# Whole plain groups beside the making of input sums, values x scores in alternating halves, and low parts of weights on VectorE

## The chip, the cores and the metric

One Trainium2 chip, one of its cores. The metric is the device time of the program in microseconds: 606.63 us in the median of three runs (605.3 to 607.45).

## What is computed

Three layers in a row, all in float32. First a decaying causal attention over 2 batches, 8 heads, 768 positions and 64 channels, in blocks of 64 positions:

```python
intra = einsum('bhic,bhjc->bhij', qb, kb) * Dmask          # Dmask = lam^(i-j), lower triangle
intra = einsum('bhij,bhjd->bhid', intra, vb)
inter = einsum('bhid,bhde->bhie', qb * lam_pow, kv_state)
out   = intra + inter
kv_state = lam_block * kv_state + einsum('bhsd,bhse->bhde', kb * rev_pow, vb)
```

Its output, as 1536 tokens of 512 features, goes through two layers of the same shape (512 to 2048 to 512):

```python
h = x @ w_in;  g = h * tanh(softplus(h));  x = g @ w_out      # first layer, mish
h = x @ w_in;  g = h * sigmoid(h);         out = g @ w_out    # second layer, silu
```

## The kernel before, in words

**Numbers in two parts.** TensorE multiplies float32 in a fast form that keeps the high bits of each operand. Every operand of the two layers is therefore held as a high part (a cast by ScalarE, L178, L402, L475) and a low part (the rest, a subtraction of the high part: L179 for weights, L403 for activations, L478 for x), and a product is three passes: high x high, low x high, high x low. The names end in h and l: `xh`/`xl` for the input tokens, `wh`/`wl` for weights, `th`/`tl` for differences of weights, `gh`/`gl` for activations, `sh`/`sl` for sums of inputs. Weights come as 64-bit numbers and are made into 32-bit ones by five VectorE instructions a tile (`split_op`, L122 to L138; in the second layer ScalarE does the first, L94).

**Tiles.** Tokens come in three tiles of 512 (t = 0, 1, 2), the 2048 hidden features of a layer in 16 slices of 128 (n), four slices to a group. There are eight groups, 0 to 7, four for each layer. A pair p is two slices, 2p and 2p + 1. `emit_h` (L418) makes the hidden values of one slice and one token tile in 12 matmuls into one PSUM bank, `activate` (L399 to L403) its activation with high and low part, `emit_o` (L441) multiplies it by the output weights in 12 matmuls into four banks that add up over a group, and `evac` (L457) adds the four banks to the output sums. Here an `emit_h` or an `emit_o` is called an item.

**Seven products instead of eight.** For token tiles 0 and 1 and a pair, the product of a 2 x 2 block matrix of x and a 2 x 2 block matrix of weights is made with seven block products instead of eight (class `Block`, L528 to L594, products by L549, six matmuls each). This needs four sums of the inputs (`sums`: made by `make_sums`, L508, for the first layer and at the end of `evac`, L487 to L502, for the second, in steps kept in the list `summing`), four differences of each pair's weights (`sum_pair`, L164), a copy of bank a to bank b by ScalarE (L568), a copy of the fifth product (L573), and two bank additions by VectorE (L557). Pairs in `plain` (L82) go without: their hidden values are made by `emit_h`, 4 items a pair. Before the change pairs 2 and 8 are plain: the first pair of group 1 and of group 4, while the sums of the layer are being made.

**Order.** The order of every engine's work is written out by hand; each engine runs its instructions in that order. The attention (12 chunks of 128 tokens; `emit_S` scores, `emit_state` state products, `emit_O` values x scores at L350 and state x queries at L344) runs first, its last eight chunks between the items of group 0 (loop at L635). Then, for each group from 1 to 7, the list `items` (L704 to L710) is gone through. After each item come, in this order: the weight parts that were pending when the item began (`run_parts`, L173: the cast by ScalarE, the low part), one low part of x (`run_rest`), one step of the sums (`run_sums`), k split instructions of the queue `todo` (`run_split`, k from L722 to L726), and weight loads into free slots (`pump`, on SP's queue). An activation's cast and low part come at the start of the next item (`run_later`).

Group 1 and group 4 (`first`, L699) begin with four `emit_h` of the plain pair, each followed by one of `fill`: an output item left over from the group before (group 1 has two of these and two idle places) with the split of an output weight queued behind it. Then follow the seven products of the second pair with output items between them. The other groups hold two pairs of seven products.

The lines that the change touches: `plain` L82; the low part of weights L179; the loops over halves and pairs in `emit_O` L348 to L352; the parts of x and the steps of the sums in `evac` L474 to L502 and in `make_sums` L520 to L526; the last attention step L643; the lists of the groups L684 to L724.

Of the kernel before, what the change touches and what calls it, by code (L numbers as in the profile page):

```python
# [7 lines left out]
F32 = mybir.dt.float32  # L8
# [9 lines left out]
def decay_attention_mish_silu_kernel(  # L18
# [60 lines left out]
    parts = []  # L79

    pre = []
    plain = (2, NF // 2)  # L82
    silu = []
    uses = {}

# [87 lines left out]
    def run_parts(k=None):  # L173
        for _ in range(len(parts) if k is None else min(k, len(parts))):
            hi, lo, f, key = parts.pop(0)
            ready.add(key)
            used(key)
            nc.scalar.copy(hi, f)  # L178
            nc.gpsimd.tensor_tensor(out=lo, in0=f, in1=hi.bitcast(F32), op=ALU.subtract)  # L179

    def run_split(k):
        for _ in range(min(k, len(todo))):
# [155 lines left out]
    def emit_O(n):  # L338
        c = n % CPS
        vn = nat.pop(n)[3]  # L340
        px = ps_a.tile([P, NP, C], F32, tag="a", name="px")
        if c > 0:
            for p in range(NP):
                nc.tensor.matmul(  # L344
                    px[:, p, :], lhsT=states[n % 2][:, p, :], rhs=qd[n][:, p, :],
                    start=(p == 0), stop=False, skip_group_check=True,
                )
        for hh in range(2):  # L348
            for p in range(NP):
                nc.tensor.matmul(  # L350
                    px[64 * hh : 64 * hh + 64, p, :], lhsT=vn[:, 2 * p + hh, :], rhs=sm[n][:, hh, p, :],
                    start=(c == 0 and p == 0), stop=(p == NP - 1), skip_group_check=True,  # L352
                )
        xslots.append(held.pop(("x", n)))
        xh, xl = x_tile(n // CPB)
        o = slice((n % CPB) * C, (n % CPB + 1) * C)
        xf = wk.tile([P, T], F32, tag="wa", name="xf").rearrange("p (a c) -> p a c", a=NP)
        nc.scalar.copy(xf, px)
        nc.scalar.copy(xh[:, :, o], xf)  # L359

        def finish():
            (nc.vector if n < PH else nc.gpsimd).tensor_tensor(out=xl[:, :, o], in0=xf, in1=xh[:, :, o].bitcast(F32), op=ALU.subtract)

        return finish
# [82 lines left out]
    def cast(i, f):  # L447
        return lambda: nc.scalar.copy(sums[i][0], f)
# [8 lines left out]
    def evac(mm, g, t):  # L457
        if g == 0:
            accs[mm, t] = (accp if t == 0 else late[1]).tile([P, 4, T], F32, tag="acc", name="acc")
        acc = accs[mm, t]  # L460
        for j in range(4):
            if g == 0:
                nc.scalar.copy(acc[:, j, :], po[t][j])
            else:
                nc.vector.tensor_tensor(out=acc[:, j, :], in0=po[t][j], in1=acc[:, j, :], op=ALU.add)  # L465
            if g == NG - 1 and mm == 1:
                r0 = t * T + j * P
                nc.sync.dma_start(out[r0 : r0 + P, :], acc[:, j, :])
        if g < NG - 1 or mm == 1:
            return  # L470

        xh, xl = x_tile(t)

        def part(j):  # L474
            nc.scalar.copy(xh[:, j, :], acc[:, j, :])  # L475
            rest.append((
                (t, j),
                lambda: nc.gpsimd.tensor_tensor(  # L478
                    out=xl[:, j, :], in0=acc[:, j, :], in1=xh[:, j, :].bitcast(F32), op=ALU.subtract
                ),  # L480
            ))

        if t != 1:
            for j in range(4):
                part(j)
            return
        a1, a2 = accs[0, 0], acc  # L487

        f1 = late[0].tile([P, 2, T], F32, tag="t4", name="s1", bufs=1)
        f3, f4 = a2[:, 0:2], a1[:, 2:4]  # L490
        add, sub = ALU.add, ALU.subtract
        drain = lambda: run_rest(len(rest))
        summing.extend([
            [tt(f1, a2[:, 0:2], a2[:, 2:4], add)],
            [cast(0, f1), lambda: part(0), lambda: part(1)],
            [low(0, f1), lambda: part(2), lambda: part(3), tt(f1, f1, a1[:, 0:2], sub)],
            [drain, cast(1, f1), tt(f4, f4, f1, sub)],
            [low(1, f1), tt(f3, a1[:, 0:2], f3, sub)],
            [cast(2, f3)],
            [low(2, f3)],  # L500
        ])
        last_sum.append([cast(3, f4), low(3, f4)])  # L502
# [5 lines left out]
    def make_sums():  # L508

        x0, x1 = x_tile(0), x_tile(1)  # L510
        sh, sl = [late[0].tile([P, 3, 2, T], F32R, tag=t, name=t, bufs=1) for t in ("sh", "sl")]
        sums.extend((sh[:, i], sl[:, i]) for i in range(3))
        sums.append((x1[0][:, 0:2], x1[1][:, 0:2]))
        q = lambda xt, k: [xt[i][:, 2 * k : 2 * k + 2].bitcast(F32) for i in (0, 1)]
        a11, a12, a21, a22 = q(x0, 0), q(x0, 1), q(x1, 0), q(x1, 1)
        tmp = late[1].tile([P, 4, T], F32, tag="acc", name="tmp")
        f1, f2 = tmp[:, 0:2], tmp[:, 2:4]
        f3 = late[0].tile([P, 2, T], F32, tag="t4", name="s3", bufs=1)
        add, sub = ALU.add, ALU.subtract
        summing.extend([  # L520
            [tt(f1, a21[0], a22[0], add), tt(f1, f1, a21[1], add), tt(f1, f1, a22[1], add), tt(f2, f1, a11[0], sub)],
            [cast(0, f1), tt(f2, f2, a11[1], sub), tt(f3, a11[0], a21[0], sub), tt(f3, f3, a11[1], add), low(0, f1)],
            [cast(1, f2), tt(f1, a12[0], f2, sub), tt(f1, f1, a12[1], add), tt(f3, f3, a21[1], sub), low(1, f2)],
            [cast(2, f3), low(2, f3)],
        ])
        last_sum.append([cast(3, f1), low(3, f1)])  # L526

    class Block:  # L528

# [105 lines left out]
    for i, (t, f) in enumerate(steps):  # L635
# [6 lines left out]
            make_sums()  # L642
        if i == len(steps) - 1:  # L643
            split_pair(3)
            sum_pair(3)
        for half in halves.get(i, ()):
            split_w(*half)
        if n < N:
# [29 lines left out]
    for g in range(1, 2 * NG):  # L678
        n0 = g * GF
        pa = n0 // 2  # L680
        A, B = Block(pa), Block(pa + 1)
        o = lambda t, f, a=False, b=False: lambda: emit_o(t, n0 + f, a, b)

        os = [(0, 0), (0, 1), (0, 2), (0, 3), (1, 1), (1, 0), (1, 3), (1, 2)]  # L684
        if g == 1:
            os = os[4:] + os[:4]
        os = [o(t, f, i % 4 == 0, i % 4 == 3) for i, (t, f) in enumerate(os)]
        hs = [lambda n=n0 + f: emit_h(2, n) for f in range(GF)]
        sp = lambda fn, *a: lambda: fn(*a)
        more = pa + 2 < NF  # L690
        nxt = [[lambda p=p: split_pair(p)] if p < NF else [] for p in (pa + 2, pa + 3)]
        if nxt[0]:
            nxt[0].append(lambda: sum_pair(pa + 2))
        fill = [[fn, sp(split_w, n0 + j, 1)] for j, fn in enumerate(fills + [idle] * (4 - len(fills)))]
        first = g in (1, NG)
        if g > 1:
            fill[0].append(lambda: sum_pair(pa + 1))
        fill[3] += nxt[0]
        if first:  # L699

            order = ((1, 1), (1, 0), (0, 0), (0, 1)) if g == 1 else ((0, 0), (0, 1), (1, 1), (1, 0))
            ha = [[lambda t=t, n=n0 + f: emit_h(t, n)] for t, f in order]
            ha[1 if g == 1 else 3].append(lambda: summing.append(last_sum.pop()))
            items = [it for i in range(4) for it in (ha[i], fill[i])]  # L704
        else:
            items = [[A.m1], [A.m5], fill[0], [A.m2], [A.m6], fill[1], [A.m7], [A.m3], fill[2], [A.m4], fill[3]]
        items += [
            [B.m1], [B.m5], [B.m2], [B.m6], [os[0]], [B.m7], [B.m3], [os[1]], [B.m4], [os[2]], [os[3]],
            [hs[0]], [os[4]], [hs[1], *nxt[1]], [os[5]], [hs[2]], [os[6]], [hs[3]], [os[7]],
        ]  # L710
        for at, item in enumerate(items):
            if g == NG and at == 7:
                silu.append(True)
            run_later()
            k = len(parts)
            for fn in item:
                fn()
            run_parts(k)
            run_rest(0 if g == NG and 7 <= at < 14 else 1)
            run_sums(1)  # L720
            small = isinstance(getattr(item[0], "__self__", None), Block)
            k = 1 if small else 0 if item[0] is idle else 3 if item[0] in hs or at < (18 if first else 11) else 2  # L722
            if g == NG and at < 8:
                k = (0, 1, 1, 1, 1, 3, 3, 3)[at]  # L724
            elif g == NG - 1 and at == len(items) - 1:
                k = 0  # L726
            run_split(k)
            pump()
        fills = [lambda n=n0 + f: emit_o(2, n, n % GF == 0, n % GF == GF - 1) for f in range(GF)]
# [49 lines left out]
```

## Time and profile before

| what | value |
|---|---|
| median of three runs | 606.63 us (605.3 to 607.45) |
| profiled execution, its own time | 607.67 us |
| its span, first to last instruction | 605.9 us |
| TensorE busy (matmul) | 575.0 us, 95% |
| VectorE busy | 418.2 us, 69% |
| ScalarE busy | 239.2 us, 39% |
| GpSimd busy | 325.5 us, 54% |
| mean granted TensorE clock | 0.979 |

The profile is one execution. PE is TensorE's matmuls, PEld its weight loads, DVE is VectorE, ACT ScalarE, POOL GpSimd, SP the engine that issues the loads. A group of instructions is named by line, engine, operation and tiles (out<-in). In brackets behind a row of a timeline stands how long the engine had been idle before it, and which instruction ended that. The duration of a matmul overlaps the next one's, so the pace of TensorE is read from starts, not from durations.

### The profile page before, as it was taken

To read this page: it belongs to the slowest core of one execution; us is meant where nothing else is said; L and a number is where in the kernel's file an instruction comes from. 1 tells how busy PE (TensorE), PEld (TensorE's weight loads), DVE (VectorE), ACT (ScalarE), POOL (GpSimd) and SP (SyncE) were. 2 spreads that over 40 slices of the span, in tenths; PEclk is the share of its full clock that TensorE was granted. 3 is DMA by queue.
4 is the path that set the end of the run, shared out by engine and by line. 5 is a ranking of instruction groups with operands and counts; after the bars stand their busy time and mean duration, and the time that the engine had idled before them with its cause. 6 is when DMAs were issued, how large, how long until landed. Compare 5 with 4: busy or idle time off the path is not lost. (4 is left out here: it accounts for less than half of the span.)

```text
span 605.9 us, 7515 instructions
## 1 busy us (share of the span) xinstructions
PE 575.0 (95%) x2870; PEld 469.3 (77%) x2870; DVE 418.2 (69%) x520; ACT 239.2 (39%) x439; POOL 325.5 (54%) x237
## 2 busy tenths in 40 slices
PE   7899999997899999999999859999999999999997
PEld 4777778886678888888887647788788878888886
DVE  3898963799858687768797779838834895567102
ACT  2435442436413334324426244446433542353220
POOL 1758783346446365646494548737554646445320
PEclk8999999999989999999999879999999999999999
DMA  7955720012322122312221112222402131200103
GB/s 253 421 179 165 288 70 1 1 35 70 104 67 73 36 69 76 98 36 70 70 70 36 35 35 70 69 70 70 133 6 70 46 102 62 70 1 1 70 0 138
DMA packets 14627, 50.55 MB, mean 83 GB/s; under 512 B 1528, under 2 KB 3072, under 8 KB 13312
## 3 DMA queue, kind: packets, MB, share of 16 engines
q1 hardware_dynamic: 14592, 50.08, 24.3%
q8 instruction: 22, 0.36, 0.2%
q14 instruction: 13, 0.11, 0.1%
HBM read 46.92 MB, written 3.15 MB: 83 GB/s over the span
## 5 line engine op out<-in xcount | busy, mean ns | idle before, releaser
L403 POOL TENSOR_TENSOR gl<-wa,gh 128x512 fp32r<-128x512 f32 x96 | 143.8, 1504 | 130.6 <-ACT gh L402 49.1
L179 POOL TENSOR_TENSOR wl<-dec,wh 128x512 fp32r<-128x512 f32 x64 | 88.4, 1381 | 84.9 <-ACT wh L178 84.8
L465 DVE TENSOR_TENSOR acc<-po,acc 128x512 f32<-128x512 f32 x72 | 46.4, 685 | 73.8 <-PE po L441 73.8
L399 ACT ACTIVATE wa<-ph 128x512 f32<-128x512 f32 x48 | 28.8, 599 | 154.2 <-PE ph L418 138.6
L441 PE MATMUL po<-gh,wh 128*128 128x512 f32 x192 | 76.8, 400 | 1.3 <-ACT wh L178 1.3
L418 PE MATMUL ph<-xl,wh 128*128 128x512 f32 x192 | 73.8, 392 | 4.0 <-POOL xl L478 4.0
L441 PE MATMUL po<-gh,wl 128*128 128x512 f32 x192 | 76.1, 396 | 0.9 <-POOL wl L179 0.9
L138 DVE SCALAR_TENSOR_TENSOR dec<-slot,dec 128x512 uint32<-128x512 uint32 x64 | 74.8, 1168 | 1.9
L418 PE MATMUL ph<-xh,wh 128*128 128x512 f32 x192 | 75.7, 394 | 0.2 <-ACT xh L359 0.2
L441 PE MATMUL po<-wl,gh 128*128 128x512 f32 x192 | 74.8, 390 | 0.9 <-POOL wl L179 0.9
L441 PE MATMUL po<-wh,gl 128*128 128x512 f32 x192 | 74.7, 389 | 0.0
L441 PE MATMUL po<-wh,gh 128*128 128x512 f32 x192 | 74.7, 389 | 0.0
L132 DVE TENSOR_SCALAR dec<-dec 128x512 f32<-128x512 f32 x64 | 47.4, 740 | 34.7 <-ACT dec L94 33.6
L136 DVE SCALAR_TENSOR_TENSOR dec<-slot,dec 128x512 uint32<-128x512 uint32 x64 | 60.6, 947 | 2.1
L402 ACT CAST gh<-wa 128x512 fp32r<-128x512 f32 x96 | 58.4, 623 | 1.1
L178 ACT CAST wh<-dec 128x512 fp32r<-128x512 f32 x64 | 39.6, 619 | 44.7 <-DVE dec L138 44.7
L418 PE MATMUL ph<-xh,wl 128*128 128x512 f32 x192 | 53.5, 393 | 0.0
L441 PE MATMUL po<-gl,wh 128*128 128x512 f32 x192 | 51.9, 392 | 0.0
L134 DVE TENSOR_SCALAR dec<-dec 128x512 uint32<-128x512 uint32 x64 | 49.7, 777 | 2.0
L179 POOL TENSOR_TENSOR tl<-t,th 128x512 fp32r<-128x512 f32 x24 | 33.6, 1408 | 24.6 <-ACT th L178 21.0
L418 PEld LDWEIGHTS ph<-xl,wh 128*128 128x128 f32 x192 | 36.0, 188 | 13.0 <-POOL xl L478 5.7
L441 PEld LDWEIGHTS po<-gh,wh 128*128 128x128 f32 x192 | 36.7, 191 | 10.3 <-ACT wh L178 1.7
(106 smaller groups left out, 962.2 us busy)
## 6 DMA issues: line engine op xcount, KB each, us to landing
slot<-w SPq DMA_DIRECT2D x64, 512.0 KB, 3.7
xslot<-x SPq DMA_DIRECT2D x10, 1024.0 KB, 9.0
out<-acc SPq DMA_DIRECT2D x12, 256.0 KB, 2.1
xslot<-x SPq DMA_DIRECT2D x4, 512.0 KB, 4.4
dmask<-scr SPq DMA_DIRECT2D x2, 256.0 KB, 4.5
lamrow<-scr SPq DMA_DIRECT2D x2, 128.0 KB, 6.7
pw<-lam SPq DMA_DIRECT2D x1, 0.0 KB
scr<-pw SPq DMA_DIRECT2D x1, 8.0 KB
```

The lines of the kernel that those rows point to most:

```text
L132: nc.vector.tensor_scalar(out=df, in0=df, scalar1=2.0**-15, scalar2=None, op0=ALU.max)
L134: nc.vector.tensor_scalar(out=d, in0=d, scalar1=3, scalar2=0x3FFFFFF8, op0=shl, op1=band)
L136: nc.vector.scalar_tensor_tensor(out=d, in0=low, scalar=29, in1=d, op0=shr, op1=bor)
L138: nc.vector.scalar_tensor_tensor(out=d, in0=high, scalar=0xC0000000, in1=d, op0=band, op1=bor)
L178: nc.scalar.copy(hi, f)
L179: nc.gpsimd.tensor_tensor(out=lo, in0=f, in1=hi.bitcast(F32), op=ALU.subtract)
L399: nc.scalar.activation(a, ps, AF.Mish if mm == 0 else AF.Silu)
L402: nc.scalar.copy(gh, a)
L403: nc.gpsimd.tensor_tensor(out=gl, in0=a, in1=gh.bitcast(F32), op=ALU.subtract)
L418: nc.tensor.matmul(ph, lhsT=wi[wsel][:, kk * P : (kk + 1) * P], rhs=xt[xsel][:, kk, :], start=(i == 0), stop=(i == 3 * KD - 1),)
L441: nc.tensor.matmul(po[t][j], lhsT=lhsT, rhs=rhs, start=(first and wsel + gsel == 0), stop=(last and gsel == 1))
L465: nc.vector.tensor_tensor(out=acc[:, j, :], in0=po[t][j], in1=acc[:, j, :], op=ALU.add)
```

## The change

Pairs 3 and 9 join the plain ones, so that groups 1 and 4 have no block products: after the `emit_h` of token tile 0 with the fills come those of tile 1, each followed by an output item of tile 0. The weight differences of the next group's first pair are queued later. The sums are taken in another order: the parts of x of tile 1 go first, the steps of the sums two places later, and the fourth sum of the first layer is made from the second at the end. Low parts of weights and of their differences move from GpSimd to VectorE. In `emit_O` the loops are exchanged, so that neighbouring matmuls write different halves of the partitions. The split counts k of the groups change with the lists.

```diff
-    plain = (2, NF // 2)
+    plain = (2, 3, NF // 2, NF // 2 + 1)
...
             nc.scalar.copy(hi, f)
-            nc.gpsimd.tensor_tensor(out=lo, in0=f, in1=hi.bitcast(F32), op=ALU.subtract)
+            nc.vector.tensor_tensor(out=lo, in0=f, in1=hi.bitcast(F32), op=ALU.subtract)
...
-        for hh in range(2):
-            for p in range(NP):
+        for p in range(NP):
+            for hh in range(2):
                 nc.tensor.matmul(
                     px[64 * hh : 64 * hh + 64, p, :], lhsT=vn[:, 2 * p + hh, :], rhs=sm[n][:, hh, p, :],
...
-        def part(j):
+        for j in range(4):
             nc.scalar.copy(xh[:, j, :], acc[:, j, :])
             rest.append((
                 (t, j),
-                lambda: nc.gpsimd.tensor_tensor(
+                lambda j=j: nc.gpsimd.tensor_tensor(
...
-            for j in range(4):
-                part(j)
             return
...
         summing.extend([
+            [], [drain],
             [tt(f1, a2[:, 0:2], a2[:, 2:4], add)],
-            [cast(0, f1), lambda: part(0), lambda: part(1)],
-            [low(0, f1), lambda: part(2), lambda: part(3), tt(f1, f1, a1[:, 0:2], sub)],
-            [drain, cast(1, f1), tt(f4, f4, f1, sub)],
+            [cast(0, f1)],
+            [low(0, f1), tt(f1, f1, a1[:, 0:2], sub)],
+            [cast(1, f1), tt(f4, f4, f1, sub)],
...
-            [cast(1, f2), tt(f1, a12[0], f2, sub), tt(f1, f1, a12[1], add), tt(f3, f3, a21[1], sub), low(1, f2)],
+            [cast(1, f2), tt(f3, f3, a21[1], sub), low(1, f2)],
             [cast(2, f3), low(2, f3)],
         ])
-        last_sum.append([cast(3, f1), low(3, f1)])
+
+        def fourth():
+            f4 = late[0].tile([P, 2, T], F32, tag="t4", name="s4", bufs=1)
+            h2, l2 = (s.bitcast(F32) for s in sums[1])
+            for fn in (tt(f4, a12[0], h2, sub), tt(f4, f4, a12[1], add), tt(f4, f4, l2, sub)):
+                fn()
+            summing.append([cast(3, f4), low(3, f4)])
+
+        last_sum.append([fourth])
...
             split_pair(3)
-            sum_pair(3)
...
-        os = [(0, 0), (0, 1), (0, 2), (0, 3), (1, 1), (1, 0), (1, 3), (1, 2)]
-        if g == 1:
-            os = os[4:] + os[:4]
+        first = g in (1, NG)
+        os = [(0, 0), (0, 1), (0, 2), (0, 3)] + [(1, f) for f in (range(4) if first else (1, 0, 3, 2))]
...
-        if nxt[0]:
+        if nxt[0] and not first:
             nxt[0].append(lambda: sum_pair(pa + 2))
...
-        if g > 1:
+        if not first:
             fill[0].append(lambda: sum_pair(pa + 1))
         fill[3] += nxt[0]
         if first:
-
-            order = ((1, 1), (1, 0), (0, 0), (0, 1)) if g == 1 else ((0, 0), (0, 1), (1, 1), (1, 0))
-            ha = [[lambda t=t, n=n0 + f: emit_h(t, n)] for t, f in order]
-            ha[1 if g == 1 else 3].append(lambda: summing.append(last_sum.pop()))
-            items = [it for i in range(4) for it in (ha[i], fill[i])]
+            hp = [[lambda t=t, n=n0 + f: emit_h(t, n)] for t in range(2) for f in range(GF)]
+
+            hp[-1].append(lambda: summing.append(last_sum.pop()))
+            items = [it for i in range(4) for it in (hp[i], fill[i])]
+            items += [it for i in range(4) for it in (hp[4 + i], [os[i]])]
+            items.append([hs[0], lambda: sum_pair(pa + 2)])
         else:
...
-            run_rest(0 if g == NG and 7 <= at < 14 else 1)
+            run_rest(0 if g == NG and 7 <= at < 12 else 1)
...
-            k = 1 if small else 0 if item[0] is idle else 3 if item[0] in hs or at < (18 if first else 11) else 2
+            k = 1 if small else 0 if item[0] is idle else 3 if item[0] in hs or at < (8 if first else 11) else 2
             if g == NG and at < 8:
-                k = (0, 1, 1, 1, 1, 3, 3, 3)[at]
+                k = (1, 1, 1, 2, 2, 2, 2, 2)[at]
```

## Rows read from the trace of the kernel before

**Rows 1.** The page, part 1: busy time of each engine, share of the span, instructions.

```profile
PE 575.0 (95%) x2870; PEld 469.3 (77%) x2870; DVE 418.2 (69%) x520; ACT 239.2 (39%) x439; POOL 325.5 (54%) x237
```

**Rows 2.** Table by stretches: length, busy PE, PEld, DVE, ACT, POOL, clock, DMA, GB/s.

```profile
140.00:172.00 32.00, 26.51 (x101) 20.70 (x99) 24.35 (x31) 13.66 (x25) 19.30 (x14) 0.89 0.26 85
172.00:320.00 148.00, 148.00 (x654) 122.56 (x653) 112.71 (x147) 54.05 (x95) 82.90 (x58) 1.00 0.20 65
320.00:390.00 70.00, 58.15 (x236) 45.80 (x235) 55.85 (x53) 31.16 (x54) 43.96 (x29) 0.93 0.16 53
```

**Rows 3.** Chain that ended last: start, us, what (twelve matmuls of one item).

```profile
443.46 2.72 PE ph L418 x12
```

**Rows 4.** Timeline of TensorE in group 1: start, us, instruction, idle before.

```profile
144.08 0.61 PE L549 MATMUL a<-xh,wh 128*128 128x512 f32 x2
...
150.30 1.07 PE L549 MATMUL a<-xh,wh 128*128 128x512 f32 x2 [3.35 <-ACT b L568]
...
165.71 0.50 PE L441 MATMUL po<-gh,wh 128*128 128x512 f32 x1 [1.25 <-ACT wh L178]
...
174.04 0.39 PE L418 MATMUL ph<-xh,wh 128*128 128x512 f32 x1
```

**Rows 5.** Timeline of ScalarE in group 1, ahead of the copy to b.

```profile
148.00 0.62 ACT L178 CAST wh<-dec 128x512 fp32r<-128x512 f32 x1 [3.44 <-DVE dec L138]
148.53 0.59 ACT L399 ACTIVATE wa<-ph 128x512 f32<-128x512 f32 x1
```

**Rows 6.** Timeline of TensorE in group 4.

```profile
331.80 0.39 PE L418 MATMUL ph<-xh,wh 128*128 128x512 f32 x1
...
339.54 0.63 PE L441 MATMUL po<-gh,wh 128*128 128x512 f32 x1
...
358.69 1.22 PE L549 MATMUL a<-xh,wh 128*128 128x512 f32 x2 [7.03 <-ACT b L568]
...
376.62 0.50 PE L441 MATMUL po<-wl,gh 128*128 128x512 f32 x1 [0.85 <-POOL wl L179]
...
381.44 0.50 PE L418 MATMUL ph<-xl,wh 128*128 128x512 f32 x1 [0.41 <-POOL xl L478]
...
382.71 0.39 PE L441 MATMUL po<-wh,gh 128*128 128x512 f32 x1
```

**Rows 7.** Table by stretches, one stretch of the attention stage.

```profile
60.00:80.00 20.00, 18.89 (x140) 15.10 (x139) 19.54 (x25) 7.21 (x16) 16.61 (x14) 1.00 0.65 250
```

**Rows 8.** Timeline of TensorE in the attention stage (px L350 is values x scores).

```profile
14.75 0.63 PE L350 MATMUL px<-sm,xslot 128*64 128x128 f32 x2
14.97 0.47 PE L326 MATMUL pc<-xslot,kd 128*64 128x64 f32 x2
...
60.39 1.58 PE L350 MATMUL px<-sm,xslot 128*64 128x128 f32 x16
...
64.85 1.16 PE L305 MATMUL s<-xslot 64*128 64x128 f32 x16
...
70.06 0.69 PE L326 MATMUL pc<-xslot,kd 128*64 128x64 f32 x16 [1.11 <-DVE sm L307]
```

**Rows 9.** Timeline of VectorE in group 4.

```profile
326.74 1.23 DVE L452 TENSOR_TENSOR sl<-s,sh 128x1024 fp32r<-128x1024 f32 x1 [2.56 <-ACT sh L448]
...
334.22 2.29 DVE L452 TENSOR_TENSOR sl<-s,sh 128x1024 fp32r<-128x1024 f32 x1
...
340.17 0.69 DVE L136 SCALAR_TENSOR_TENSOR dec<-slot,dec 128x512 uint32<-128x512 uint32 x1
```

**Rows 10.** Timeline of GpSimd in group 4.

```profile
330.34 7.30 POOL L478 TENSOR_TENSOR xl<-acc,xh 128x512 fp32r<-128x512 f32 x4
```

**Rows 11.** Groups by line: busy us, mean ns of one, idle before, releaser.

```profile
L179 POOL TENSOR_TENSOR wl<-dec,wh 128x512 fp32r<-128x512 f32 x64 | 88.4, 1381 | 84.9 <-ACT wh L178 84.8
```

**Rows 12.** One line of the kernel, L362: duration in ns (least, median, most), first and last start.

```profile
L362 POOL TENSOR_TENSOR xl<-xf,xh x8: 1268/1295/1590, 39.8 to 104.6; 128x512 fp32r<-128x512 f32 x8
L362 DVE TENSOR_TENSOR xl<-xf,xh x4: 684/738/995, 16.9 to 32.8; 128x512 fp32r<-128x512 f32 x4
```

More of the change, by code (lines that the diff above doesn't have):

```diff
@@ L691, in decay_attention_mish_silu_kernel @@
         nxt = [[lambda p=p: split_pair(p)] if p < NF else [] for p in (pa + 2, pa + 3)]
-        if nxt[0]:
+        if nxt[0] and not first:
             nxt[0].append(lambda: sum_pair(pa + 2))
         fill = [[fn, sp(split_w, n0 + j, 1)] for j, fn in enumerate(fills + [idle] * (4 - len(fills)))]
-        first = g in (1, NG)
-        if g > 1:
+        if not first:
             fill[0].append(lambda: sum_pair(pa + 1))
@@ L699, in decay_attention_mish_silu_kernel @@
         if first:
-            order = ((1, 1), (1, 0), (0, 0), (0, 1)) if g == 1 else ((0, 0), (0, 1), (1, 1), (1, 0))
-            ha = [[lambda t=t, n=n0 + f: emit_h(t, n)] for t, f in order]
-            ha[1 if g == 1 else 3].append(lambda: summing.append(last_sum.pop()))
-            items = [it for i in range(4) for it in (ha[i], fill[i])]
+            hp = [[lambda t=t, n=n0 + f: emit_h(t, n)] for t in range(2) for f in range(GF)]
[3 more added lines that the diff above has]
+            items.append([hs[0], lambda: sum_pair(pa + 2)])
         else:
             items = [[A.m1], [A.m5], fill[0], [A.m2], [A.m6], fill[1], [A.m7], [A.m3], fill[2], [A.m4], fill[3]]
[L707 to L710, printed above, removed]
+            items += [
+                [B.m1], [B.m5], [B.m2], [B.m6], [os[0]], [B.m7], [B.m3], [os[1]], [B.m4], [os[2]], [os[3]], [hs[0]],
+            ]
+        items += [[os[4]], [hs[1], *nxt[1]], [os[5]], [hs[2]], [os[6]], [hs[3]], [os[7]]]
         for at, item in enumerate(items):
```

## The prediction, made before the changed kernel ran

> **What bounds the kernel now.** The busy table comes first [rows 1]: TensorE is busy 95% of the span, VectorE 69%, GpSimd 54%. Busy does not mean flat out, so the second view is the table by stretches [rows 2]: from 172 to 320 us TensorE is busy all the time at clock 1.00, while from 140 to 172 us it is busy 26.51 of 32 us at 0.89, and from 320 to 390 us 58.15 of 70 at 0.93. These two stretches hold the groups in which the input sums of the two layers are made. The third view, the chain that ended last, gives the price of undisturbed work: a run of 12 matmuls, one hidden or output item, takes 2.72 us [rows 3], 0.2267 us each.
>
> With that price the timeline of TensorE shows what each stretch loses. In group 1, from 144.08 to 174.04 us, run the seven products of pair 3 (42 matmuls) and four output items (48): 90 x 0.2267 = 20.40 us of work in 29.96 us, so **9.56 us are lost** [rows 4]. The largest wait is 3.35 us of product a on ScalarE's copy to b; after it two matmuls take 1.07 us instead of 0.61, the lower clock level of 1.2 GHz that the 0.89 stands for. The copy was late because ScalarE, which works in order, had sat 3.44 us before a weight cast that VectorE's fifth split instruction was to release [rows 5]. In group 4, from 331.80 to 382.71 us, are nine items and seven products, 150 matmuls or 34.00 us, in 50.91 us: **16.91 us are lost** [rows 6]. The first item alone took 339.54 - 331.80 = 7.74 us instead of 2.72, waiting for low parts of x that GpSimd makes; then came 7.03 us on the same copy.
>
> In the attention stage VectorE is the other limit: 19.54 of 20 us between 60 and 80 us [rows 7], and TensorE waited 1.11 us for its masked scores [rows 8].
>
> **The change, part by part.** The profiled execution took 607.67 us, 1.04 above the median of 606.63; the sum is made against 607.67.
>
> Pairs 3 and 9 become plain. Each gives up 7 products x 6 = 42 matmuls for 4 items x 12 = 48: 12 more matmuls, 12 x 0.2267 = **+2.72 us**, straight on the path. Gone with them are 8 differences, 4 bank additions, 4 ScalarE copies and 4 low parts, all beside TensorE.
>
> Group 1 then holds no product at all, so the copy that product a waited for does not exist there. The sums, which used to be due at the first products of the second pair, are now due a whole group later, some 20 items or 54 us. What could still stall is weights: bounded by 0 and by the 2.88 us that the output item at 165.71 us lost [rows 4] (174.04 - 165.71 = 8.33 us for two items of 5.44). Counting the split instructions that the items hand out, the first output weight of the group is complete at the fourth item and used at the tenth, the last at the twelfth and used at the sixteenth; two or more items of 2.72 us cover the cast, the low part and the wait. I take 0: **-9.56 us**.
>
> Group 4 loses its products likewise. The first use of token tile 1 moves from the fifth item to the ninth, 4 x 2.72 = 10.9 us later, and the four casts and low parts of that tile now go ahead of the sums in ScalarE's and GpSimd's queues. Against that, the low parts of tile 2 are due after the sixteenth item, three items sooner in the list of items than before, and GpSimd must place the last behind a low part of an activation. So **-16.91 us**, and new waits between 0 and the waits on low parts that the stretch shows today: 5.02 + 0.85 + 0.41 = 6.28 us [rows 6]. VectorE was busy 55.85 us of the 70 here [rows 2]; the new stage has 24 items, 65.3 us, and VectorE fits on the mean. But seven sum instructions of 1024 columns stand in its first eight items, each 1.23 us alone and 2.29 beside GpSimd [rows 9, 10]: VectorE will run a few us late when the bank evacuation of tile 2 comes, and an output item waits for those banks. I take one late bank and one late low part, **+2.5 us**, nearer the small rows than the large one.
>
> Values x scores in alternating halves. These 16 matmuls of 64 output columns take 1.58 us in two runs of one half each; the 16 score matmuls, which alternate halves of the rows, take 1.16 [rows 8]. At 14.97 us state products of the next chunk, which alternate halves of the columns, start while the last values x scores of the chunk before, begun at 14.75, still run: two column halves work side by side [rows 8]. The bounds are 0 and half of 1.58, 0.79 us a chunk; I take the score row, the one with as many moving columns: 1.58 - 1.16 = 0.42. The first four chunks stay behind VectorE and DMAs; the other eight give 3.4 us, of which I count **-3.0**, since VectorE's queue is as full there as TensorE's. The matmuls now need both score halves from the second on; VectorE writes both before TensorE arrives, except where it is late already.
>
> The Trainium skill, TensorE: Matmul & The Clock Gate, Part 3 (The mechanism), speaks against this: it says a weight load overlaps running matmuls only when the row group differs, and both halves here use all rows. By that rule this part gives nothing and the sum is 3.0 us higher. The state products that start inside the other half's work, on the same rows, do not look like it [rows 8].
>
> Low parts of weights to VectorE. After the change there are 64 + 20 = 84. One costs GpSimd 1.38 us [rows 11]; the same shape on both engines (low part of x) takes 0.738 us on VectorE and 1.295 on GpSimd, by the medians [rows 12]. VectorE gains 84 x 0.74 = 62 us of work, and GpSimd, with the 4 that vanish, loses 88 x 1.38 = 121. But the two engines mostly exclude each other: the 1.23 us subtraction takes 2.29 while GpSimd's four low parts run at 1.8 us each instead of 1.3 [rows 9, 10, 12], so each GpSimd instruction beside it costs VectorE 2.29 - 1.23 = 1.06 us. Where both are full, VectorE comes out 0.3 us ahead for each low part; the cover holds on the mean. The new wait is that VectorE, in order, stands until ScalarE has cast the high part, behind it the next split instructions, bank additions and evacuations, and behind those TensorE. An activation that itself waits for TensorE's item can stand ahead of the cast. Bounds: 0, and the cast of 0.62 us [rows 5] shown in full 84 times, 52 us. From 172 to 320 us VectorE idles a quarter of the time [rows 2], and a bank addition has one output item of 2.72 us before the next product is due: activation and cast (0.59 + 0.62 [rows 5]), low part 0.74 and one split instruction 0.69 [rows 9] make 2.64 us after the product ahead, which ends 1.36 us sooner still. I take **0**. The weight DMAs keep their order on SP's queue; their slots come free at the same split instruction.
>
> Sum: 607.67 - 9.56 - 16.91 + 2.72 - 3.0 + 2.5 = 583.4 us; less 1.04 for the median: **582.4 us**.
>
> **The rivals.** (a) VectorE's queue binds in the attention stage: ten low parts of 0.74 us enter a queue that has no idle time [rows 7], GpSimd's relief does not reach it, and the halves bring nothing: +7.4 + 3.0, 592.8 us. For it: 19.54 of 20 us. Against: 10 x 1.06 us less lock. (b) Group 4 keeps its waits on low parts in full (6.28 instead of 2.5), and group 1 the 2.88 us on weights: +6.7, 589 us. For it: seven sums and the splits in eight items. (c) Nothing new waits, halves give 0.79 and the attention waits vanish: -2.5 - 3.3, some 576.5 us. (d) The late copy was never due to the sums but to ScalarE behind VectorE, and moves to the first products of the next groups: 3.35 + 7.03 us come back with their slow matmuls (1.2 + 1.4), some 595 us. Against: those groups had no wait before [rows 2]. (e) Slower: VectorE waits for a cast at every low part and TensorE for VectorE. The price is 84 x 0.62 = 52 us, 634 us; the point at which the gain of 24 us is gone is 0.29 us a low part. It decides if VectorE has no slack in the plain stretches; it was busy 112.71 of 148 us there [rows 2], which speaks against it. By the Trainium skill's rule on weight loads, without the 3.0 us, the time is 585.4, inside the forecast's spread.
>
> **How the numbers follow.** Forecast (577 to 588) 0.60; (c) 0.11; (a) and (b) together 0.18; (d) 0.05; (e) or a milder form of it 0.04; no change 0.02, if several go wrong at once. A measurement here tells about 0.3%, 1.8 us, from no change. The range 576 to 592 takes in the forecast, most of (b) and the edges of (a) and (c), about 0.8. Faster 0.94, same 0.02, slower 0.04.
>
> **What would show it.** Right: groups 1 and 4 at clock 1.00 in the table by stretches, items 2.72 us apart, no wait on the copy to b; the 16 values x scores near 1.16 us; GpSimd near 204 us busy. Wrong: waits of TensorE on VectorE's low parts, bank additions or masked scores; a row of VectorE's low parts with ScalarE's cast as the releaser and TensorE idle at the same time; item gaps in groups 2 and 5.

## The result and the profile after

The changed kernel takes **597.47 us** (median of four runs, 596.38 to 597.66), the kernel before beside it 607.04: ratio 0.984, interval 0.981 to 0.987. That is 1.6% faster; 582.4 us was forecast, and the time lies outside the range. The profiled execution took 597.66 us.

The page, part 1, of the changed kernel; it answers to [rows 1].

```profile
PE 572.8 (96%) x2882; PEld 466.5 (78%) x2882; DVE 426.5 (72%) x593; ACT 236.7 (40%) x431; POOL 203.8 (34%) x149
```

The table by stretches, with the columns of [rows 2]: one early stretch; most of group 1; its end with groups 2 and 3; most of group 4.

```profile
20.00:40.00 20.00, 14.87 (x132) 11.97 (x129) 19.19 (x29) 6.28 (x15) 8.20 (x7) 0.83 0.81 317
...
140.00:180.00 40.00, 37.43 (x159) 30.59 (x158) 34.37 (x47) 15.07 (x27) 12.54 (x8) 0.96 0.26 82
180.00:320.00 140.00, 137.69 (x606) 113.06 (x605) 110.26 (x161) 50.38 (x89) 43.06 (x30) 1.00 0.21 67
320.00:385.00 65.00, 62.38 (x268) 51.17 (x267) 51.95 (x62) 33.04 (x55) 29.86 (x19) 0.97 0.18 58
```

The work moved as foreseen: 12 more matmuls, GpSimd at 204 us. The copy to b no longer holds groups 1 and 4. But TensorE has new gaps: in groups 2 and 3, which were full before, and at one place each in groups 1 and 4; and in the attention stage a gap that it had has become longer. From the table of waits of the changed kernel (us in total, times, longest), those of TensorE whose longest has grown, and VectorE's waits for ScalarE's casts:

```profile
PE px L350 <- DVE sm L307: 5.1, 3, 4.1
PE ph L418 <- POOL xl L478: 2.6, 1, 2.6
PE po L441 <- DVE acc L465: 2.6, 1, 2.6
...
PE b L555 <- DVE c L563: 2.3, 2, 1.2
PE pc L326 <- DVE sm L307: 1.9, 1, 1.9
```

```profile
DVE wl L179 <- ACT wh L178: 37.4, 41, 1.8
...
DVE tl L179 <- ACT th L178: 9.5, 8, 2.8
```

All but one of TensorE's name VectorE: masked scores (sm), the evacuation of banks (acc), a bank addition (c). Where they stand, from the timeline of TensorE:

```profile
30.62 2.57 PE L350 MATMUL px<-sm,xslot 128*64 128x128 f32 x16 [4.07 <-DVE sm L307]
33.12 2.08 PE L305 MATMUL s<-xslot 64*128 64x128 f32 x16
...
62.62 0.69 PE L326 MATMUL pc<-xslot,kd 128*64 128x64 f32 x16 [1.86 <-DVE sm L307]
...
85.42 1.09 PE L350 MATMUL px<-sm,xslot 128*64 128x128 f32 x16
...
167.82 0.39 PE L418 MATMUL ph<-xh,wh 128*128 128x512 f32 x1
...
173.27 0.79 PE L441 MATMUL po<-gh,wh 128*128 128x512 f32 x1 [2.57 <-DVE acc L465]
...
177.70 0.39 PE L418 MATMUL ph<-xh,wh 128*128 128x512 f32 x1
...
219.96 0.39 PE L441 MATMUL po<-gh,wh 128*128 128x512 f32 x1
...
224.00 0.73 PE L555 MATMUL b<-sh,th 128*128 128x512 f32 x2 [1.16 <-DVE c L563]
...
365.78 0.39 PE L418 MATMUL ph<-xh,wh 128*128 128x512 f32 x1
...
370.15 0.50 PE L418 MATMUL ph<-xl,wh 128*128 128x512 f32 x1 [2.62 <-POOL xl L478]
...
375.75 0.39 PE L418 MATMUL ph<-xh,wh 128*128 128x512 f32 x1
```

With 2.72 us an item the losses can be read off: group 1, 177.70 - 167.82 - 5.44 = 4.44 us; group 4, 375.75 - 365.78 - 5.44 = 4.53; group 2, 224.00 - 219.96 - 2.72 = 1.32, and the same in group 3. After the 4.07 us wait the clock is down (0.50 between 30 and 35 us, the level of 1.2 GHz): the 16 values x scores take 2.57 us against 1.09 at 85.42, the scores 2.08 against 1.16 [rows 8]. In the kernel before, the same wait took 2.12 us:

```profile
28.91 1.69 PE L350 MATMUL px<-sm,xslot 128*64 128x128 f32 x16 [2.12 <-DVE sm L307]
```

How a low part makes an evacuation late shows in group 1. VectorE's timeline first, then ScalarE's:

```profile
166.50 0.69 DVE L179 TENSOR_TENSOR wl<-dec,wh 128x512 fp32r<-128x512 f32 x1 [1.53 <-ACT wh L178]
167.10 1.22 DVE L455 TENSOR_TENSOR s<-xh,sh 128x1024 f32<-128x1024 f32 x1
168.36 2.20 DVE L455 TENSOR_TENSOR s<-s,xl 128x1024 f32<-128x1024 f32 x1
...
172.53 2.48 DVE L465 TENSOR_TENSOR acc<-po,acc 128x512 f32<-128x512 f32 x4
```

```profile
165.36 0.60 ACT L399 ACTIVATE wa<-ph 128x512 f32<-128x512 f32 x1 [3.81 <-PE ph L418]
165.85 0.61 ACT L178 CAST wh<-dec 128x512 fp32r<-128x512 f32 x1
```

The cast at 165.85 stands behind an activation that waits for TensorE's item. VectorE, idle since 164.97, waits 1.53 us for it, then has the low part, the three steps of the fourth input sum, which the change puts there (1.22, 2.20 and 1.23 us), and two split instructions in front of the evacuation. TensorE left the item to be evacuated at 167.82; VectorE begins at 172.53, and the next output item waits for its banks.

### The profile page after: what moved, and what is told of

The parts are those of the page before. It is cut to its first block, busy times and chain, and to the rows that moved or that the text cites. A ratio compares the mean times of both kernels' runs of the same rounds, so it can differ in the third digit from the quotient of the medians.

```text
span 595.9 us, 7472 instructions
## 1 busy us (share of the span) xinstructions
PE 572.8 (96%) x2882; PEld 466.5 (78%) x2882; DVE 426.5 (72%) x593; ACT 236.7 (40%) x431; POOL 203.8 (34%) x149
## 5 line engine op out<-in xcount | busy, mean ns | idle before, releaser
L418 PE MATMUL ph<-xh,wh 128*128 128x512 f32 x224 | 88.7, 396 | 0.0
L418 PE MATMUL ph<-xl,wh 128*128 128x512 f32 x224 | 85.9, 390 | 2.6 <-POOL xl L478 2.6
L399 ACT ACTIVATE wa<-ph 128x512 f32<-128x512 f32 x56 | 33.5, 598 | 138.0 <-PE ph L418 131.7
L179 DVE TENSOR_TENSOR wl<-dec,wh 128x512 fp32r<-128x512 f32 x64 | 49.1, 767 | 37.8 <-ACT wh L178 37.4
L138 DVE SCALAR_TENSOR_TENSOR dec<-slot,dec 128x512 uint32<-128x512 uint32 x64 | 63.1, 985 | 1.9
L136 DVE SCALAR_TENSOR_TENSOR dec<-slot,dec 128x512 uint32<-128x512 uint32 x64 | 62.2, 971 | 2.1
L418 PE MATMUL ph<-xh,wl 128*128 128x512 f32 x224 | 61.8, 391 | 0.0
L132 DVE TENSOR_SCALAR dec<-dec 128x512 f32<-128x512 f32 x64 | 44.7, 698 | 21.8 <-ACT dec L94 20.7
L418 PEld LDWEIGHTS ph<-xl,wh 128*128 128x128 f32 x224 | 42.1, 188 | 11.6 <-POOL xl L478 3.0
L418 PEld LDWEIGHTS ph<-xh,wh 128*128 128x128 f32 x224 | 42.4, 189 | 9.7 <-issue 0.2
L418 PEld LDWEIGHTS ph<-xh,wl 128*128 128x128 f32 x224 | 42.3, 189 | 8.7
```

Source lines behind the costliest of these rows:

```text
L132: nc.vector.tensor_scalar(out=df, in0=df, scalar1=2.0**-15, scalar2=None, op0=ALU.max)
L136: nc.vector.scalar_tensor_tensor(out=d, in0=low, scalar=29, in1=d, op0=shr, op1=bor)
L138: nc.vector.scalar_tensor_tensor(out=d, in0=high, scalar=0xC0000000, in1=d, op0=band, op1=bor)
L179: nc.vector.tensor_tensor(out=lo, in0=f, in1=hi.bitcast(F32), op=ALU.subtract)
L399: nc.scalar.activation(a, ps, AF.Mish if mm == 0 else AF.Silu)
L418: nc.tensor.matmul(ph, lhsT=wi[wsel][:, kk * P : (kk + 1) * P], rhs=xt[xsel][:, kk, :], start=(i == 0), stop=(i == 3 * KD - 1),)
```

## The experiments

Every ratio is to the kernel before, run beside it on the same chip (medians 607.2 to 607.8 us).

**1. Low parts of weights back on GpSimd**, all else as changed.

```diff
-            nc.vector.tensor_tensor(out=lo, ...)
+            nc.gpsimd.tensor_tensor(out=lo, ...)
```

> The changed kernel with the low parts of weights back on GpSimd, nothing else undone. Theory 1 (low parts in VectorE's own queue make masked scores, bank additions and evacuations late): the 4.1 and 1.9 us waits on masked scores, the 2.6 us wait on the evacuation in group 1 and the two 1.2 us waits on bank additions go, the wait on low parts of x in group 4 grows from 2.6 us to 4 to 6: 586 to 591 us. Rival (what VectorE gains in own work it loses in waits for GpSimd, so the place of the low parts does not matter): 596 to 599 us.

587.29 us, 0.967 (0.965 to 0.970): theory 1. The move cost the changed kernel 10.2 us. The last values x scores of the attention start at 100.00 us instead of 104.10; groups 2 and 3 are full again, group 1 loses 0.5 us; group 4 loses 6.0 us instead of 4.5, on two waits for low parts of x, which is the one place where the move helped. By the two profiles, the move cost 4.1 us in the attention stage, 3.9 in group 1 and 2.6 in groups 2 and 3, and gave 1.5 back in group 4.

**2. Only the low parts on VectorE**, in the kernel before.

```diff
-            nc.gpsimd.tensor_tensor(out=lo, ...)
+            nc.vector.tensor_tensor(out=lo, ...)
```

> The kernel before with only the low parts of weights moved to VectorE. Theory 1: the attention stage loses some 5 us and groups 2 and 3 some 3 us, while groups 1 and 4 keep most of their waits: 609 to 615 us, slower than before. Rival (low parts on VectorE relieve the pair of engines, the losses come from the plain groups and the halves): 600 to 606 us.

610.58 us, 1.006 (1.004 to 1.008): some 3 us slower by itself. The two losses of 1.32 us in groups 2 and 3 appear here too, and the last values x scores start at 106.02 us, 4.4 later than before. In group 1, by contrast, TensorE loses 7.2 us instead of 9.5: there the move helped.

**3. Only the halves**, in the kernel before: the two loops of `emit_O` exchanged.

```diff
-        for hh in range(2):
-            for p in range(NP):
+        for p in range(NP):
+            for hh in range(2):
```

> The kernel before with only the values x scores in alternating halves. If the halves run side by side at the score row's price: eight chunks by 0.45 us, 603 to 604 us. By the rule that weight loads do not overlap within one row group: 607 us. If the need for both score halves at the start costs more than it brings: 608 us or more.

604.96 us, 0.995 (0.994 to 0.997), a gain of some 2.5 us (interval 1.8 to 3.9). Sixteen of these matmuls took 1.09 us, less than the 1.16 of the score row.

**4. Low parts on GpSimd while the attention runs**, then on VectorE.

```diff
-            nc.vector.tensor_tensor(out=lo, ...)
+            (nc.vector if late else nc.gpsimd).tensor_tensor(out=lo, ...)
```

> The changed kernel with the low parts of weights on GpSimd until the attention is over and on VectorE from then on. Theory 1: only the waits on masked scores go, with the slow matmuls behind the longest: some 5 us, 591 to 594 us. Rival (the waits on masked scores come from the alternating halves, which need both score halves, or from the loads of x): 596 to 598 us.

593.04 us, 0.976 (0.973 to 0.979): 4.4 us of the 10.2 come back. In the profiled execution, the longest of the four (594.31 us), the last values x scores start 2.2 us earlier than in the changed kernel, and the waits of values x scores for masked scores add up to 3.7 us instead of 5.1: shorter, but not gone. Groups 1 to 3 lose about what they lose in the changed kernel (group 1 4.8 us). Group 4 loses 2.9 us instead of 4.5, behind a wait of the same length (2.64 and 2.62 us) and with the same instructions: here the clock is 1.00 from 367 to 374 us, in the changed kernel it was 0.76 from 369 to 376. So the attention stage has some 2 to 4 us of the 10.2, and the clock behind one and the same wait is worth 1.5 us from one execution to the next.

**5. Low parts on VectorE, one place later.** The cast is issued where it was; the low part waits in a list that is emptied ahead of the next item or the next casts.

```diff
             nc.scalar.copy(hi, f)
-            nc.vector.tensor_tensor(out=lo, ...)
+            lows.append((hi, lo, f, key))      # emptied at the next run_later or run_parts
```

> The changed kernel; the low parts stay on VectorE, but each is issued one place later (ahead of the next item or the next casts), so that ScalarE's cast lies behind split instructions that are issued in between. If VectorE's waits for casts (47 us in all) are what costs: most of the 10 us between the changed kernel and the one with low parts on GpSimd come back, 588 to 591 us. If it is the low parts' own time in a queue that is already late (57 us of work, whatever their place): 595 to 598 us.

588.54 us, 0.969 (0.966 to 0.972). The same 84 instructions on the same engine, and 8.9 of the 10.2 us are back. VectorE's waits for casts fell from 46.9 to 21.4 us in the table of waits:

```profile
DVE wl L187 <- ACT wh L177: 16.1, 15, 3.4
DVE tl L187 <- ACT th L177: 5.3, 5, 1.2
```

The attention stage hardly moved (last values x scores at 103.66 us). Group 1 loses 0.9 us, groups 2 and 3 0.4 each, group 4 2.2. So in groups 1 to 3 it was the wait in the queue: 5.4 of the 6.6 us that the move cost there are back. Another 2.3 us of the 8.9 come from group 4, where the move had cost nothing. In the attention stage, where VectorE has no idle time to wait in (19.19 of 20 us busy), it was something else.

**6. Low parts of x of token tile 2 earlier** in group 4, in the changed kernel.

```diff
-            run_rest(0 if g == NG and 7 <= at < 12 else 1)
+            run_rest(1)
```

> The changed kernel; in group 4 the low parts of x of token tile 2 are given to GpSimd from the eighth item on, one an item, instead of from the thirteenth. GpSimd stood idle between 338 and 355 us. If only their late issue made TensorE wait: the 4.5 us lost at the seventeenth item go, 593 us. If GpSimd cannot place them for lack of the shared path to memory: 596 to 598 us.

593.95 us, 0.978 (0.976 to 0.980): 3.5 of the 4.5 us. Group 4 then loses 0.8 us, on a low part of weights.

**7. Experiments 1 and 6 together.**

```diff
-            nc.vector.tensor_tensor(out=lo, ...)
+            nc.gpsimd.tensor_tensor(out=lo, ...)
...
-            run_rest(0 if g == NG and 7 <= at < 12 else 1)
+            run_rest(1)
```

> Low parts of weights on GpSimd and the low parts of x of token tile 2 issued early, both edits in one. If the two losses are separate: 587.3 less 6.0 = 581 us, which is the sum that the prediction made. If GpSimd's low parts of weights push the early ones back: 585 to 588 us.

**583.94 us**, 0.962 (0.960 to 0.965), 13.5 us under the changed kernel and 1.5 above the forecast. Behind the attention no single item loses more than 0.8 us.

**8. Plain groups and the order of the sums alone**: the changed kernel with its two other parts undone.

```diff
-            nc.vector.tensor_tensor(out=lo, ...)
+            nc.gpsimd.tensor_tensor(out=lo, ...)
...
-        for p in range(NP):
-            for hh in range(2):
+        for hh in range(2):
+            for p in range(NP):
```

> The kernel before with the plain groups and the order of the sums alone, low parts of weights on GpSimd and the halves in turn. If the parts add: 587.3 plus the 2.5 to 2.9 us of the halves, 590 us. If the halves only pay where VectorE is not late: 588 us.

590.07 us, 0.972 (0.969 to 0.974): 17 us gained. The halves, which experiment 1 has besides, add 2.8 us to it, near the 2.5 that they give alone.

**9. Experiments 5 and 6 together**, their two edits as shown.

> The changed kernel with both mends: low parts of weights on VectorE one place later, low parts of x of token tile 2 on GpSimd from the eighth item of group 4 on. The 2.0 us that the seventeenth item still loses there goes, part of it to VectorE's low parts that wait for GpSimd: 586 to 588 us. If VectorE's queue in group 4 is full, 589 or more.

589.18 us, 0.969 (0.968 to 0.971): a miss, and the time of the other reading. An output item in group 4 loses 4.1 us waiting for a low part of weights. Ahead of it, beside GpSimd's early low parts of x and one of an activation, three of VectorE's split instructions take 1.53, 1.40 and 1.66 us and the low part 1.74; the mend of one queue is taken back in the other.

**10. First four chunks with the halves in turn**, one after the other as before the change, in the kernel of experiment 7.

```diff
-        for p in range(NP):
-            for hh in range(2):
+        pairs = [(p, hh) for p in range(NP) for hh in range(2)]
+        if n < PH:
+            pairs.sort(key=lambda q: q[1])
+        for p, hh in pairs:
```

> Low parts of weights on GpSimd, low parts of x early, and the first four chunks with the halves in turn as in the kernel before, the other eight alternating. If the need for both masked scores lengthens the wait of the fourth chunk: 0.5 to 1.5 us less than 583.9, 582.5 to 583.5 us. If the alternating order gains in the first chunks too: 584 to 586 us.

583.95 us, 0.961 (0.959 to 0.962): the same time as experiment 7; neither reading is told from the other by the time. The wait of the fourth chunk stayed at 1.94 us, so it is not the need for both masked scores that makes it; in experiment 7 the second of them added 0.16 us.

**11. Low parts on GpSimd in the attention, then on VectorE one place later**, with experiment 6: to experiment 9 comes the edit of experiment 4. While the attention runs, each low part is issued right behind its cast.

```diff
-            nc.vector.tensor_tensor(out=lo, ...)
+            (nc.vector if late else nc.gpsimd).tensor_tensor(out=lo, ...)
```

> Low parts of weights on GpSimd until the attention is over, then on VectorE one place later; low parts of x of token tile 2 early. If what is left with GpSimd's low parts (3.3 us lost in single waits behind the attention) comes from GpSimd: 582 to 583 us. If VectorE's queue takes its place: 584 to 587 us.

586.24 us, 0.965 (0.963 to 0.967): 2.3 us over experiment 7. Even with the wait mended VectorE is the worse place for these instructions behind the attention; 2.5 us are lost in one output item of group 4 that waits for a low part.

## Why the prediction was wrong

**The step that failed** is the last part, "Low parts of weights to VectorE", which the forecast took at 0, between bounds of 0 and 52 us. It cost 10.2 us in the changed kernel (experiment 1 against the changed kernel) and 3.1 alone (experiment 2, interval 2.4 to 4.8); most of the difference lies in group 1, where it saved 2.4 us alone and cost 3.9 in the changed kernel. The step named the wait for the cast and the activation ahead of it, but covered it with one case, a bank addition that came right behind one low part and one split instruction. Two things were left out. VectorE arrives at that place late already. In group 2 of the changed kernel it works without a pause from 209.5 to 221.6 us and begins an evacuation at 215.83, 1.4 us after TensorE has gone on; then come a low part, five split instructions, a second low part with its wait for the cast, one more split instruction and the addition. TensorE was ready for the sum at 222.68 us (219.96 + 2.72); the addition began at 223.25:

```profile
215.83 2.48 DVE L465 TENSOR_TENSOR acc<-po,acc 128x512 f32<-128x512 f32 x4
...
222.31 0.69 DVE L179 TENSOR_TENSOR wl<-dec,wh 128x512 fp32r<-128x512 f32 x1 [0.69 <-ACT wh L178]
222.91 0.42 DVE L130 TENSOR_SCALAR dec<-slot 128x512 uint32<-128x512 uint32 x1
223.25 0.69 DVE L563 TENSOR_TENSOR c<-b,m 128x512 f32<-128x512 f32 x1
```

And a mean idle share of a quarter is no cover. Before, VectorE used it to run ahead of TensorE; for the same evacuation it had been waiting 2.18 us:

```profile
215.72 2.48 DVE L465 TENSOR_TENSOR acc<-po,acc 128x512 f32<-128x512 f32 x4 [2.18 <-PE po L441]
```

A low part that hangs on an activation ties VectorE to TensorE's pace at that point, and the lead is gone. Issued one place later, the same low parts leave these waits nearly gone (experiment 5).

**The sum of the miss.** From 582.4 to 597.47 are 15.1 us: 10.2 for this step, 3.5 for group 4 (6.0 us lost in experiment 1 instead of 2.5), 0.5 for group 1 and 0.2 to 0.5 for the halves; another 0.4 is that the kernel before, run beside the changed one, took 607.04 us and not the 606.63 that the forecast started from.

**The attention stage** was to give 3.0 us and lost 2.0 (the last values x scores start 2.5 us later, and end 0.5 us sooner after their start). The halves gave their part, 2.5 to 2.8 us by experiments 3 and 8: that term was right in kind and near in size. The rest is the same failed step, rival (a): 4.1 us between the changed kernel and experiment 1 at that point, by one profile of each. VectorE's timeline ahead of the fourth chunk's masked scores, in the changed kernel:

```profile
25.20 1.42 DVE L138 SCALAR_TENSOR_TENSOR dec<-slot,dec 128x512 uint32<-128x512 uint32 x1
26.54 0.84 DVE L130 TENSOR_SCALAR dec<-slot 128x512 uint32<-128x512 uint32 x1
27.41 1.37 DVE L132 TENSOR_SCALAR dec<-dec 128x512 f32<-128x512 f32 x1
28.82 0.43 DVE L134 TENSOR_SCALAR dec<-dec 128x512 uint32<-128x512 uint32 x1
29.16 0.68 DVE L179 TENSOR_TENSOR wl<-dec,wh 128x512 fp32r<-128x512 f32 x1
29.88 1.29 DVE L307 TENSOR_TENSOR sm<-s,dmask 128x512 f32<-128x512 f32 x2
```

In the kernel before, the same masked scores began at 28.17 us, and three of these split instructions took 0.69, 0.42 and 0.43 us:

```profile
25.17 0.69 DVE L138 SCALAR_TENSOR_TENSOR dec<-slot,dec 128x512 uint32<-128x512 uint32 x1
25.78 0.42 DVE L130 TENSOR_SCALAR dec<-slot 128x512 uint32<-128x512 uint32 x1
26.23 0.43 DVE L132 TENSOR_SCALAR dec<-dec 128x512 f32<-128x512 f32 x1
26.69 1.44 DVE L134 TENSOR_SCALAR dec<-dec 128x512 uint32<-128x512 uint32 x1
28.17 1.29 DVE L307 TENSOR_TENSOR sm<-s,dmask 128x512 f32<-128x512 f32 x2
```

So 0.68 of the 1.71 us is the low part itself; the rest is split instructions, three of which are now longer and one shorter. With the move alone (experiment 2) those three take 1.42, 0.84 and 1.37 us as well, so it is the move that makes them longer. The longer ones lie beside instructions of GpSimd, before as now. GpSimd's queue used to stand at a low part that waited for its cast, and now runs its attention work through. Its timeline in the kernel before, and in the changed one:

```profile
22.81 1.77 POOL L294 TENSOR_TENSOR qd<-xslot,lamrow 128x512 f32<-128x512 f32 x1
26.59 1.26 POOL L179 TENSOR_TENSOR wl<-dec,wh 128x512 fp32r<-128x512 f32 x1 [2.00 <-ACT wh L178]
```

```profile
24.57 1.49 POOL L313 TENSOR_TENSOR state<-state,lamrow 128x512 f32<-128x512 f32 x1
26.03 1.07 POOL L282 TENSOR_TENSOR kd<-xslot,dmask 128x256 f32<-128x256 f32 x1
27.06 1.44 POOL L294 TENSOR_TENSOR qd<-xslot,lamrow 128x512 f32<-128x512 f32 x1
```

The prediction counted 1.06 us of relief for each low part taken off GpSimd; here there was none, because other work of GpSimd took the place. That reading rests on the timelines; no run separates its cost from the low part's own time.

**Plain groups and sums.** The forecast was -9.56 - 16.91 + 2.72 + 2.5 = -21.3 us; alone they gave 17. The copy to b did vanish, as said, and the matmuls cost what was said. Group 4 is the mis-sized term: 5.5 and 0.4 us lost in experiment 8 instead of 2.5, nearly the upper bound of 6.28. The wait is the one named, the low parts of x of tile 2, but GpSimd was not short of time: in the changed kernel it was busy 4.33 of the 17 us from 338 to 355, and the code held these instructions back until the thirteenth item. GpSimd's timeline, with a low part of an activation and the first and the last of these four:

```profile
351.61 1.29 POOL L403 TENSOR_TENSOR gl<-wa,gh 128x512 fp32r<-128x512 f32 x1 [5.38 <-ACT gh L402]
...
357.00 1.74 POOL L478 TENSOR_TENSOR xl<-acc,xh 128x512 fp32r<-128x512 f32 x1
...
368.66 1.44 POOL L478 TENSOR_TENSOR xl<-acc,xh 128x512 fp32r<-128x512 f32 x1
```

The step priced the collision and overlooked the release; experiments 6 and 7 are that release, worth 3.5 and 3.4 us.

**Group 1** was taken as free of waits, with weights as the only candidate. No weight was late; the evacuation was, and group 1 lost 4.44 us, in experiment 1 0.5. The prediction's words "behind it the next split instructions, bank additions and evacuations" named the evacuation; then only the addition was priced.

**The rule on weight loads** (the Trainium skill, TensorE: Matmul & The Clock Gate, Part 3 (The mechanism)) as the prediction applied it would have the halves gain nothing, since both use all rows. 16 such matmuls went from 1.58 to 1.09 us, and the kernel gained 0.5% (experiment 3): the measurement differs, and decides. The rows of before differ from the rule too: from 172 to 320 us TensorE's matmuls fill all of the 148 us, and its weight loads, which there use all 128 rows, are busy for 122.56 of the same 148 [rows 2]: by these rows, in which the ends of matmuls are modelled, they overlap running matmuls. The prediction's own sign, state products that start before the last values x scores end, proves little, since a matmul's duration overlaps the next one's anyway. Why the alternating order is faster, no run shows.

**The rivals.** (e) came nearest in kind, at 10.2 / 84 = 0.12 us a low part instead of 0.62 and short of its point of 0.29; (a) and (b) each came true in part; (d) did not, since no wait on a copy is new: one of 0.5 us in group 5 stood there before too; (c) was ruled out by the new waits.

## What to carry to other kernels

A cross-engine wait put into an in-order queue is to be priced by everything behind it up to the next thing TensorE needs, at each place where it falls, not by its own length or by the engine's mean idle share. If the producer stands behind an instruction that itself waits for TensorE, issue the consumer later in the queue: the same instructions one place later made the kernel 8.9 us faster, within 1.3 us of the one without the move. When an engine's queue is relieved, ask what it runs instead, and against whom; and when an item waits for an engine that is idle, look for the line that holds its work back.

## What was not expected

GpSimd takes about twice as long for a low part, and is still the better engine for it: 583.94 us, against 586.24 for the best arrangement that has the low parts on VectorE behind the attention. The groups of instructions in experiment 1 (busy us in total and mean ns of one; then the idle time of the engine before them):

```profile
L179 POOL TENSOR_TENSOR wl<-dec,wh 128x512 fp32r<-128x512 f32 x64 | 89.6, 1400 | 94.4 <-ACT wh L178 94.4
L179 POOL TENSOR_TENSOR tl<-t,th 128x512 fp32r<-128x512 f32 x20 | 27.5, 1384 | 19.0 <-ACT th L178 15.5 <-issue 3.5
```

The mean one takes 1.40 us, against 0.77 for wl on VectorE in the changed kernel, and GpSimd stands for ScalarE's casts 109.9 us, more than VectorE's 46.9. The likely reason why it costs less is that less of what TensorE needs soon is queued behind it; no run shows this by itself, and in group 4, where low parts of x are queued there, TensorE does wait (6.0 us in experiment 1).
